# Eight-row blocks for the triangular inverse on VectorE, several operations merged, and a new written order of the work

## The chip, the cores and the metric

One core of one Trainium2 chip runs the whole program. The metric is the time of one execution on the device in microseconds; lower is better. The core has four engines that matter here: TensorE (PE in the profile; its weight loads are PEld), VectorE (DVE), ScalarE (ACT) and GpSimd (POOL). SyncE (SP) issues most of the transfers from and to HBM. Each engine works through its own instructions strictly in the order in which they were written.

## The reference

A recurrent attention (a state of 40 x 40 for each of 32 pairs of batch and head, 768 steps) is followed by a mixture of 8 experts with one expert per row:

```python
for t in range(S):                       # B, H, S, D = 4, 8, 768, 40
    y[:, :, t] = einsum('bhd,bhde->bhe', r_t, state)
    Sa = einsum('bhde,bhe->bhd', state, a_t)
    state = state * w_t[:, :, None, :] - einsum('bhd,bhe->bhde', Sa, b_t)
    state = state + einsum('bhd,bhe->bhde', v_t, k_t)
x = y as rows of 320 (3072 of them)
expert = argmax(x @ w_gate)              # with a softmax weight for the row
h = max(x_rows_of_expert @ w1[e], 0)     # 320 -> 1024, at most 768 rows per expert
out[row] = weight * (h @ w2[e])          # 1024 -> 320
```

All inputs and the result are float32.

## The kernel before, in words

The 768 steps are cut into six passes (`i` from 0 to 5) of 128 steps, and each pass into two chunks of 64 (`c`). Heads are packed in two groups (`pr` 0 and 1), so each pass has four units (`pr`, `c`). Inside a chunk the 64 steps do not follow one another in time: the effect of `Sa` within a chunk is a lower triangular system of 64 x 64 for every head, and the kernel inverts that triangle.

**The steps of one pass.** `decay` and `decay_k` turn the factors `w` into running products by two scans on VectorE (L518, L527) and multiply them into `a` and `kb` (L532 and L537, on VectorE or on GpSimd). `nn` forms the triangles by matmul (L418, operands `a` and `kb`) and copies them, negated, from PSUM into `ns` (L161). `inverse` then works on the two 32 x 32 diagonal blocks of each triangle, with the 32 triangles of the pass side by side:

- L792 transposes `ns` into `xu`, so that each partition holds a whole 32 x 32 block in its 1024 elements, and VectorE can work along the partition.
- The elimination (L665 and L670, function `elim`) goes row by row through the two diagonal blocks of 16: a product of a column of `xu` with a row of `nu` into `tmp`, then a sum into `nu`. For rows with much work it is cut into two halves, listed as `inverse` and `inverse_b`, which do not depend on one another.
- Two transposes (L680, L685) bring the result back.
- `join` takes the blocks from 16 to 32 by two rounds of matmuls (`yb`, `yq` and `sw` are their operands; L736, function `take_jb`, puts the corner into `xu`), and `comb` takes them from 32 to 64 in the same way. The result is `nt`.

`chain` is the recurrence: `zz` and `chain` compute `Sa` from the state `D` or `E`, `uT`, `out` and `turn` compute the outputs and the new state. In `out` the matmuls of step `yy` take two products into one PSUM tile, one with `bk` and one with `Sd`, the turned state. `take_y` scales the output into `px` (L982) and `gate` makes the rows of 320 as a float16 pair, high and low, in `x16`, and the logits of the router. `route` makes the lists of rows, and the expert steps (`x`, `w`, `p`, `h`, `o`) gather rows and multiply by the weights; these are the last 214 us.

**What sets the order.** Every step has a function, the engines that it may run on with planned durations ("V1.97", "A.62 A.62|V.69 V.69"), and the steps and buffers that it needs. The order is not planned when the program is built: the table `ORDER` at L31 lists the steps one by one. A name is the next step of that thread, `/1` chooses the second engine, `*2` repeats, and `~3` puts three idle matmuls of 128 x 512 (function `warm`, L210) ahead of it, which fill a gap on TensorE. The buffers are few: `ns`, `xu`, `nu`, `yb` and `yq` exist once, so the inverse of one pass has to be finished with them before the next one starts.

## Time and profile before

| | us |
|---|---|
| median of 3 runs (606.46 to 618.24) | 613.48 |
| the profiled execution | 609.18 |
| its span from first to last instruction | 606.9 |
| recurrence, up to the first expert's matmuls | 0 to 393 |
| experts alone | 393 to 606.9 |

Busy time is the time in which an engine had at least one instruction; the remaining time it waited. The granted clock of TensorE was 0.975 of full speed over the span. The six inverses start (L792) at 31.8, 76.7, 134.0, 189.6, 251.3 and 308.8 us, so the passes between them took 44.9, 57.3, 55.6, 61.7 and 57.5 us.

### The profile page before, as it was taken

What the parts mean: (1) busy time and instruction counts of PE and PEld (TensorE: products, weight loads), DVE (VectorE), ACT (ScalarE), POOL (GpSimd) and SP (SyncE); (2) the same over time, 40 slices, a digit from 0 to 9 for tenths busy, and PEclk for the clock granted to TensorE, in tenths of its full rate; (3) what the DMA queues carried; (4) which work ended last, traced back from release to release, by engine and by line L of the source; (5) the groups of instructions that cost most, each with busy time, mean ns of one, the idle gap of its engine ahead of it and who ended that gap; (6) DMA issues with size and microseconds to landing.
All of it is one profiled execution on the core that took longest, in us unless ns stands there. A gap on an engine that the chain in (4) does not pass through costs nothing.

```text
span 606.9 us, 25053 instructions
## 1 busy us (share of the span) xinstructions
PE 529.7 (87%) x11167; PEld 388.4 (64%) x11167; DVE 423.5 (70%) x904; ACT 291.7 (48%) x544; POOL 156.8 (26%) x184
## 2 busy tenths in 40 slices
PE   0576789889988988998889999799899998999995
PEld 0344478778866876887678788566565553655653
DVE  6998988979897886799799489477247252551540
ACT  3133646664656476556556653165336442452431
POOL 9110003240330154111320000303422333451323
PEclk9998999999999998999899999799799998999999
DMA  7672015413630455134332422886798589693211
GB/s 227 201 227 62 2 33 161 150 53 122 191 123 12 145 157 167 53 113 153 105 98 74 150 73 60 172 199 201 197 230 185 149 199 237 161 245 88 46 55 48
DMA packets 74761, 80.82 MB, mean 133 GB/s; under 512 B 31550, under 2 KB 55232, under 8 KB 74644
## 3 DMA queue, kind: packets, MB, share of 16 engines
q1 hardware_dynamic: 71316, 69.69, 41.6%
q0 software_dynamic: 3328, 9.44, 5.8%
q8 instruction: 89, 1.46, 1.0%
q14 instruction: 28, 0.23, 0.1%
HBM read 64.16 MB, written 10.09 MB: 122 GB/s over the span
## 4 chain that ended last, share of the span: by engine, by line
PE 41%; DVE 22%; issue 13%; ACT 10%; DMA 7%; POOL 3%; SPq 2%; another core or an unknown queue 1%; POOLq 0%; DVEq 0%; ACTq 0%
PE pp L418 19%; PE pp L1632 8%; PE p L1501 5%; ACT yb L161 3%; DMA xT<-a 3%; POOL out_dram L1507 2%; DVE tmp L665 2%; DVE nu L670 2%; DVE vu L470 2%; PE pp L888 2%; PE pp L210 2%; DVE px L527 2%; DVE ns L161 1%; ACT ns L161 1%; DVE xu L736 1%
## 5 line engine op out<-in xcount | busy, mean ns | idle before, releaser
L1507 POOL DMA_INDIRECT out_dram<-tk,ri x27 | 36.1, 1336 | 103.0 <-ACT tk L1667 82.0
L418 PE MATMUL pp<-a,kb 64*64 64x64 f32 x1536 | 32.4, 227 | 24.7 <-DVE a L532 20.1
L210 PE MATMUL pp<-ident 128*128 128x512 f16 x146 | 40.8, 388 | 10.0 <-ACT ns L161 2.2
L418 PEld LDWEIGHTS pp<-a,kb 64*64 64x64 f32 x1536 | 27.5, 139 | 32.5 <-issue 27.9
L466 POOL TENSOR_SCALAR_AFFINE_SELECT tk<-tk 64x512 f32<-64x512 f32 x24 | 15.8, 657 | 103.8 <-ACT tk L463 102.8
L418 PE MATMUL pp<-vu,bk 128*40 128x104 f32 (+1 forms) x768 | 39.2, 254 | 3.3 <-issue 2.6
L537 POOL TENSOR_TENSOR kb<-kb,gx 104x1024 f32<-104x1024 f32 x13 | 29.0, 2239 | 47.1 <-DVE nu L670 18.9
L418 PEld LDWEIGHTS pp<-vu,bk 128*40 128x40 f32 x768 | 33.6, 118 | 8.4 <-issue 5.9
L1478 POOL DMA_INDIRECT a<-xd,ri x25 | 26.2, 1049 | 45.9 <-DVE gs L1393 27.9
L1640 DVE SCALAR_TENSOR_TENSOR px<-pp,rv 128x448 f16<-128x448 f32 (+1 forms) x24 | 13.8, 597 | 32.2 <-ACT rv L1637 32.2
L418 PE MATMUL pp<-yb,ns 128*64 128x64 f32 (+1 forms) x768 | 25.8, 228 | 9.5 <-ACT yb L161 9.5
L161 ACT ACTIVATE yb<-nu,few 64x512 f32<-64x512 f32 (+1 forms) x36 | 29.7, 857 | 8.8 <-DVE nu L685 8.2
L161 ACT ACTIVATE ns<-pp 32x256 f32<-32x256 f32 (+1 forms) x42 | 18.9, 451 | 30.9 <-PE pp L418 30.2
L157 ACT COPY vT<-pp 128x1024 f32<-128x1024 f32 x22 | 22.3, 1014 | 23.0 <-PE pp L888 20.8
L418 PEld LDWEIGHTS pp<-yb,ns 128*64 128x64 f32 (+1 forms) x768 | 24.0, 131 | 12.8 <-ACT yb L161 12.1
L527 DVE TENSOR_TENSOR_SCAN px<-px,z 104x1032 f32<-104x1032 f32 x12 | 31.3, 2606 | 0.4
L1632 PE MATMUL pp<-xT,px 128*128 128x448 f16 (+2 forms) x128 | 29.1, 315 | 2.4 <-issue 1.8
L470 DVE TENSOR_TENSOR vu<-pp,mask 128x1024 f32<-128x1024 f32 x22 | 26.8, 1218 | 6.2 <-PE p L926 3.7
L1632 PE MATMUL pp<-xT,xu 128*128 128x448 f16 (+2 forms) x128 | 28.5, 315 | 2.7 <-DMA xT<-a 2.7
L1637 ACT ACTIVATE rv<-pp 128x448 f16<-128x448 f32 (+2 forms) x28 | 13.1, 490 | 36.1 <-PE pp L1632 29.0
L418 PE MATMUL pp<-rv,vT 64*64 64x64 f32 x1536 | 28.4, 221 | 2.2 <-ACT vT L157 1.2
L518 DVE TENSOR_TENSOR_SCAN gx<-px,z 104x1032 f32<-104x1032 f32 x12 | 27.7, 2308 | 3.4 <-DMA px<-in_w_dram 2.7
(262 smaller groups left out, 1433.7 us busy)
## 6 DMA issues: line engine op xcount, KB each, us to landing
vu<-in_moe_w_dram SPq DMA_DIRECT2D x32, 320.0 KB
kb<-in_kb_dram SPq DMA_DIRECT2D x40, 224.0 KB
px<-in_moe_w_dram SPq DMA_DIRECT2D x16, 512.0 KB
rv<-in_rv_dram SPq DMA_DIRECT2D x24, 256.0 KB
vu<-in_vt_dram SPq DMA_DIRECT2D x48, 128.0 KB
xd<-x SPq DMA_DIRECT2D x24, 192.0 KB
a<-in_a_dram SPq DMA_DIRECT2D x16, 224.0 KB
px<-in_moe_w_dram SPq DMA_DIRECT2D x14, 256.0 KB
```

The costliest lines, as they stand in the source:

```text
L157: (e.copy if e is self.nc.scalar else e.tensor_copy)(out, in_)
L161: (e.mul if e is self.nc.scalar else e.tensor_scalar_mul)(out, in_, x)
L210: self.nc.tensor.matmul(x, self.spare[:, 0:P], self.spare[:, None, :].to_broadcast([P, 2, 2 * P]), start=True, stop=True, skip_group_check ...
L418: TT.matmul(out, l, r, start=start, stop=True, skip_group_check=True)
L470: V.tensor_mul(out, in_, m.to_broadcast(sh))
L518: V.tensor_tensor_scan(T["gx"][0:R, 0:H * (P + 1)][:, ::-1], T["px"][0:R].rearrange("p h t -> p (h t)")[:, ::-1], z2[0:R].rearrange("p h t ...
L527: V.tensor_tensor_scan(T["px"][0:R].rearrange("p h t -> p (h t)"), T["px"][0:R].rearrange("p h t -> p (h t)"), z2[0:R].rearrange("p h t -> ...
L537: engine().tensor_mul(x, x, g[:, :, None, half(c)].to_broadcast([R, H, 2, C]))
L1478: nc.gpsimd.indirect_dma_start(out=xt(j)[:c].rearrange("p a c -> p (a c)"), out_offset=None, in_=src[:, :], in_offset=bass.IndirectOffsetO ...
L1501: nc.tensor.matmul(po[z], h(l, f + z), rr(f + z, 1)[:, 0], start=(f == 0 and m == 0), stop=(f == NF - n and m == 2), skip_group_check=True)
L1507: nc.gpsimd.indirect_dma_start(out=out_v[used[0] % (8 * E)][:, :], out_offset=bass.IndirectOffsetOnAxis(ap=ri.bitcast(U32)[:c, j, 1:2], ax ...
L1632: nc.tensor.matmul(s_["h", f + z][:, :n], l, rr, start=m % 7 == 0 and m < 14, stop=m >= 14)
```

## The change: smaller blocks, merged operations, another order

What it does, by part:

1. The elimination covers four diagonal blocks of 8 instead of two of 16: six rows of a product and a sum on all four blocks at once, uncut, in place of fourteen rows, most of them cut in two. `inverse_b` is gone.
2. From 8 to 16, VectorE forms the corner itself: two products of 512 elements and a sum over groups of 8, twice (`corner_mul`, `corner_sum`). It uses the buffer `yq` for the products.
3. Pairs of instructions become one: `take_jb` (with another placing of `join_b`'s output in PSUM), `take_turn` (the copy into `Sd`), `take_y`, and the high half in `x_hi`. The factor 64 moves from `take_y` to `x_hi` and `x_lo`.
4. In `yy` the product with `Sd` goes first and the one with `bk` second.
5. `ORDER` is new from end to end, with its choices of engine and its idle matmuls (146 + 28 before, 148 + 21 now).

```diff
 ORDER = """
-load_w decay0 load_kb decay0 load_a decay_k0 load_kb load_a load_w decay_k0 decay1 load_kb inverse_0 load_kb
...
+load_kb load_w decay0 load_kb load_a decay0 load_rv load_kb load_w decay_k0 load_a load_kb inverse_0 load_w decay_k0
...
-        nb = 2 if i in SIX else 1
-        ne = 32 // nb
+        nb, ne = 4, 8
...
-            m = s + 1
-            rows = [(s + 1, ne)]
-            if nb * (ne - 1 - s) * m >= 84:
-                h = s + 1 + (ne - s) // 2
-                rows = [(s + 1, h), (h, ne)]
...
+            m, n = s + 1, ne - 1 - s
+            tv = tmp[:, 0:nb * n * m].rearrange("p (b t j) -> p b t j", b=nb, t=n)
+
+            def mul():
+                V.tensor_mul(tv, diag(s_["xu"])[:, :, s + 1:, s:s + 1].to_broadcast([P, nb, n, m]),
+                             diag(s_["nu"])[:, :, s:s + 1, 0:m].to_broadcast([P, nb, n, m]))
+
+            def add():
+                y = diag(s_["nu"])[:, :, s + 1:, 0:m]
+                V.tensor_add(y, y, tv)
+
+            return mul, add
+
+        def eight(x, b, t, s, *dims):
+            return skew(x, b * 528 + t * 32 + s, *dims)
+
+        def corner_mul(x):
+            def go():
+                if x == 0:
+                    s_["y"] = get("yq")
+                for b in range(2):
+                    if x == 0:
+                        l = eight(s_["xu"], b, 8, 0, (32, 8), (0, 8), (1, 8))
+                        r = eight(s_["nu"], b, 0, 0, (0, 8), (1, 8), (32, 8))
+                    else:
+                        l = eight(s_["nu"], b, 8, 8, (32, 8), (0, 8), (1, 8))
+                        r = skew(tmp, P + 64 * b, (0, 8), (1, 8), (8, 8))
+                    V.tensor_mul(flat(s_["y"])[:, 512 * b:512 * b + 512].rearrange("p (t j s) -> p t j s", t=8, j=8), l, r)
+            return go
+
+        def corner_sum(x):
+            def go():
+                y = flat(s_["y"])
+                if x == 0:
+                    V.tensor_reduce(tmp[:, P:], y.rearrange("p (m s) -> p m s", s=8), AX.X, ALU.add)
+                else:
+                    V.tensor_reduce(skew(s_["nu"], 256, (528, 2), (32, 8), (1, 8)),
+                                    y.rearrange("p (b t j s) -> p b t j s", b=2, t=8, j=8), AX.X, ALU.add)
+                    put("yq", s_["y"])
+            return go
...
-            for z in range(2):
-                x = s_["ntd"][half(z), :, 16:32].rearrange("p (v u) t -> p v u t", v=2)
-                y = s_["p"][half(z), ::1 - 2 * z, 0:256].rearrange("p v (u t) -> p v u t", u=16)
-                V.scalar_tensor_tensor(x, y, low[half(z), 0:1], x, ALU.mult, ALU.add)
+            x = s_["ntd"][:, :, 16:32].rearrange("p (v u) t -> p v u t", v=2)
+            y = s_["p"][:, :, 0:256].rearrange("p v (u t) -> p v u t", u=16)
+            V.scalar_tensor_tensor(x, y, low, x, ALU.mult, ALU.add)
...
+        for x in range(2):
+            add(corner_mul(x), "V1.2", take=["yq"] * (1 - x))
+            add(corner_sum(x), "V1.2", free=["yq"] * x)
...
-            for x in range(2):
-                copy(U["Sd"][:, x], pv[:, :, C * x:C * x + D])
+            copy(U["Sd"], skew(U["pd"], 0, (C, 2), (R, 4), (1, D)))
...
-            for r in range(2):
-                x = T["px"][0:R, 4 * r:4 * r + 4, ct]
-                y = p[0:R, r].rearrange("p (k y) -> p k y", k=4)[:, :, D * r:D * r + C]
-                V.scalar_tensor_tensor(x, y, SX, x, ALU.mult, ALU.mult)
+            x = T["px"][0:R, :, ct].rearrange("p (r k) t -> p r k t", r=2)
+            V.tensor_mul(x, skew(p[0:R], 0, (512 + D, 2), (P, 4), (1, C)), x)
```

Instructions that the new list puts on another engine or takes from one, counted on VectorE (before, now): `zs` copies 14, 2; `vu` copies 10, 18; `Sd` copies 32 (halves), 4 (whole), with 18 whole ones on ScalarE; `nt` copies from PSUM 10, 4; products of `a` 7, 4 (GpSimd 5, 8); scalings into `yb` 0, 8, into `sw` 0, 2, into `yq` 0, 2; mask products into `tk` 6, 7; `vT` copies 2, 3.

Three places show what the new list moves. In the rows, numbers behind a name are buffers, and line numbers are those of each file.

SP's first transfers, before: `px` is the factor `w` of a group, each row a pair of half transfers.

```order
L171 DMA px_119<-in_w_dram 128x516 x2
L171 DMA kb_129<-in_kb_dram 128x512 x2
L171 DMA a_125<-in_a_dram 128x512 x2
L171 DMA kb_129<-in_kb_dram 128x512 x2
L171 DMA a_126<-in_a_dram 128x512 x2
L171 DMA px_120<-in_w_dram 128x516 x2
L171 DMA kb_130<-in_kb_dram 128x512 x4
```

The same place in the changed kernel:

```order
L157 DMA kb_129<-in_kb_dram 128x512 x2
L157 DMA px_119<-in_w_dram 128x516 x2
L157 DMA kb_129<-in_kb_dram 128x512 x2
L157 DMA a_125<-in_a_dram 128x512 x2
L157 DMA rv_131<-in_rv_dram 128x512 x2
L157 DMA kb_130<-in_kb_dram 128x512 x2
L157 DMA px_120<-in_w_dram 128x516 x2
```

The `w` of the first group has moved from first to second place, and that of the second group from sixth to seventh.

VectorE between the second L685 of pass 0 (after `take_jb`) and the transpose that starts the inverse of pass 1, before:

```order
L161 TENSOR_SCALAR nt_141<-xu_138,few 128x16x32 x2
L525 COPY g_1_165<-gx_118 104x8
L526 RECIPROCAL z_168<-gx_118 104x8
L527 SCALAR_TENSOR_TENSOR px_122<-px_122,z_168 104x1032
L532 TENSOR_TENSOR a_128<-a_128,px_122 104x1024
L537 TENSOR_TENSOR kb_130<-kb_130,gx_118 104x1024 x2
L161 TENSOR_SCALAR ns_137<-pp_113 128x512
L161 TENSOR_SCALAR ns_137<-pp_113 32x8x32 x2
L157 COPY nt_140<-pp_115 32x16x32 x2
```

The same stretch in the changed kernel:

```order
L510 COPY g_1_165<-gx_118 104x8
L511 RECIPROCAL z_168<-gx_118 104x8
L512 SCALAR_TENSOR_TENSOR px_122<-px_122,z_168 104x1032
L147 TENSOR_SCALAR sw_136<-xu_138,few 64x512 x2
L522 TENSOR_TENSOR kb_130<-kb_130,gx_118 104x1024
L147 TENSOR_SCALAR ns_137<-pp_113 128x512
L147 TENSOR_SCALAR ns_137<-pp_113 32x8x32 x2
L147 TENSOR_SCALAR ns_137<-pp_113 128x512
L147 TENSOR_SCALAR ns_137<-pp_113 32x8x32 x2
L503 SCALAR_TENSOR_TENSOR gx_118<-px_123,z_168 104x1032
L143 COPY zs_153<-pp_114 64x8x40 x2
```

The product of `a`, one of `kb`, the two copies into `nt` at either end have left VectorE there; two for `sw` and two for `zs` have come.

GpSimd's first products, before:

```order
L537 TENSOR_TENSOR kb_130<-kb_130,gx_118 104x1024
L537 TENSOR_TENSOR kb_129<-kb_129,gx_118 104x1024
L466 AFFINE_SELECT tk_135<-tk_135 64x512 x4
```

GpSimd's first products in the changed kernel:

```order
L522 TENSOR_TENSOR kb_129<-kb_129,gx_118 104x1024 x2
L517 TENSOR_TENSOR a_127<-a_127,px_121 104x1024
L522 TENSOR_TENSOR kb_130<-kb_130,gx_118 104x1024
L517 TENSOR_TENSOR a_128<-a_128,px_122 104x1024
```

Five products of pass 1 stand there now in place of one (the first of before belongs to pass 0); over the whole program GpSimd has 21 of them where it had 18.

## Rows read from the trace of the kernel before

**Rows 1.** The page's busy times (share, instructions) and the chain by engine.

```profile
PE 529.7 (87%) x11167; PEld 388.4 (64%) x11167; DVE 423.5 (70%) x904; ACT 291.7 (48%) x544; POOL 156.8 (26%) x184
PE 41%; DVE 22%; issue 13%; ACT 10%; DMA 7%; POOL 3%; SPq 2%; another core or an unknown queue 1%; POOLq 0%; DVEq 0%; ACTq 0%
```

**Rows 2.** Stretch, length; busy PE, PEld, DVE, ACT, POOL (instructions); clock, DMA share, GB/s.

```profile
31.77:76.67 44.90, 32.89 (x693) 21.47 (x692) 40.17 (x82) 19.68 (x34) 2.18 (x1) 0.96 0.29 89
76.67:133.95 57.28, 52.50 (x1697) 44.52 (x1697) 48.50 (x107) 34.47 (x64) 15.09 (x12) 1.00 0.34 105
...
393.00:606.90 213.90, 200.12 (x1424) 119.57 (x1421) 95.55 (x174) 89.55 (x170) 68.30 (x58) 0.97 0.65 160
```

**Rows 3.** Groups by line and shape, TensorE: count, busy us, mean ns, idle before.

```profile
L210 PE MATMUL pp<-ident 128*128 128x512 f16 x146 | 40.8, 388 | 10.0 <-ACT ns L161 2.2 <-issue 2.0 <-ACT yq L157 1.2
L418 PE MATMUL pp<-vu,bk 128*40 128x104 f32 x704 | 35.7, 254 | 0.7 <-DVE vu L470 0.5
```

**Rows 4.** VectorE in order of time, start of the program: start, us, instruction.

```profile
4.61 2.31 DVE L518 TENSOR_TENSOR_SCAN gx<-px,z 104x1032 f32<-104x1032 f32 x1 [2.18 <-DMA px<-in_w_dram]
...
14.68 2.31 DVE L518 TENSOR_TENSOR_SCAN gx<-px,z 104x1032 f32<-104x1032 f32 x1 [0.52 <-DMA px<-in_w_dram]
...
19.54 4.05 DVE L527 TENSOR_TENSOR_SCAN px<-px,z 104x1032 f32<-104x1032 f32 x1
...
31.77 1.93 DVE L792 STREAM_TRANSPOSE xu<-ns 128x1024 f32<-128x1024 f32 x1 [0.26 <-ACT ns L161]
```

**Rows 5.** VectorE in order of time, the inverse of pass 0.

```profile
33.96 0.22 DVE L665 TENSOR_TENSOR tmp<-xu,nu 128x56 f32<-128x56 f32 x1
34.22 0.22 DVE L670 TENSOR_TENSOR nu<-nu,tmp 128x56 f32<-128x56 f32 x1
...
38.10 1.23 DVE L470 TENSOR_TENSOR tk<-pp,mask 128x1024 f32<-128x1024 f32 x1
...
40.31 2.23 DVE L665 TENSOR_TENSOR tmp<-xu,nu 128x60 f32<-128x60 f32 x1
...
45.46 1.97 DVE L680 STREAM_TRANSPOSE xu<-nu 128x1024 f32<-128x1024 f32 x1
47.47 1.25 DVE L685 STREAM_TRANSPOSE nu<-xu 128x1024 f32<-128x1024 f32 x1
```

**Rows 6.** GpSimd in order of time, its first two products.

```profile
19.20 2.23 POOL L537 TENSOR_TENSOR kb<-kb,gx 104x1024 f32<-104x1024 f32 x1 [3.66 <-DMA kb<-in_kb_dram]
40.28 2.18 POOL L537 TENSOR_TENSOR kb<-kb,gx 104x1024 f32<-104x1024 f32 x1 [18.85 <-DVE nu L670]
```

**Rows 7.** Groups of VectorE by line and shape: the prices.

```profile
L1370 DVE TENSOR_TENSOR tm<-lane,sp 128x512 f32<-128x512 f16 x5 | 3.4, 684 | 0.0
L1355 DVE TENSOR_TENSOR ne<-ne,oh__99 128x128 f32<-128x128 f32 x1 | 0.4, 393 | 0.0
L1346 DVE TENSOR_TENSOR ne<-p,base 128x128 f32<-128x128 f32 x1 | 0.3, 283 | 0.0
L1302 DVE TENSOR_REDUCE mx<-lg 128x16 f32<-128x128 f32 x1 | 0.3, 286 | 0.0
L157 DVE COPY Sd<-p 128x160 f32<-128x160 f32 x32 | 8.8, 317 | 0.3 <-PE p L926 0.2
L157 DVE COPY zs<-pp 64x320 f32<-64x320 f32 x14 | 6.8, 487 | 1.1 <-PE pp L418 0.8
L527 DVE TENSOR_TENSOR_SCAN px<-px,z 104x1032 f32<-104x1032 f32 x12 | 31.3, 2606 | 0.4
```

**Rows 8.** VectorE in order of time, end of pass 0 and start of pass 1.

```profile
58.16 1.51 DVE L736 SCALAR_TENSOR_TENSOR xu<-pp,few,xu 64x512 f32<-64x512 f32 x2 [1.55 <-PE pp L418]
...
65.43 2.35 DVE L537 TENSOR_TENSOR kb<-kb,gx 104x1024 f32<-104x1024 f32 x2
...
69.43 1.38 DVE L157 COPY nt<-pp 32x512 f32<-32x512 f32 x2
...
76.67 2.00 DVE L792 STREAM_TRANSPOSE xu<-ns 128x1024 f32<-128x1024 f32 x1 [1.07 <-ACT ns L161]
```

More of the change, by code (lines that the diff above doesn't have):

```diff
@@ L796, in inverse @@
         add(begin2, "V1.97", needs=[("nn", (pr, 2 * i + c)) for pr in range(2) for c in range(2)] + [("unit", i)], take=["xu"])
[L797 to L798 removed]
+        add(first, "V.2")
         for s in range(1, ne - 1):
[L800 to L805 removed]
+            for x in elim(s):
+                add(x, "V.2")
+        for x in range(2):
+            add(corner_mul(x), "V1.2", take=["yq"] * (1 - x))
+            add(corner_sum(x), "V1.2", free=["yq"] * x)
         add(back_a, "V1.94", gives=("ntd0", i))
@@ L814, in inverse @@
         add(join_b, "P1.0", needs=[("sw", i)], take=["pp"], free=["yq", "sw"])
[L815 removed]
+        add(take_jb, "V.69", free=["pp"], gives=("ntd", i))
         add(lambda: back_b(0, 1), "V1.22", gives=("n1", i))
@@ L957, in yy @@
                        True)
+            if q:
+                for k in range(4):
+                    for r in range(2):
+                        for x in range(2):
+                            mm(p[half(x, D), r, k * P + D * r:k * P + D * r + C], U["Sd"][half(r), x, k, :],
+                               T["rv"][half(r), c, x * 4 + k, :], k == 0 and not old)
+                put("Sd", U["Sd"])
             for k in range(4):
@@ L1001, in chain @@
             more(turn, "P.4", needs=[("S", pr, q)], take=["p1"], gives=("turned", n))
-            more(take_turn, "A.33 A.33|V.33 V.33", take=["Sd"], free=["p1"], gives=("Sd", n))
+            more(take_turn, "A.46|V.49", take=["Sd"], free=["p1"], gives=("Sd", n))
         more = steps(f"out{pr}")
@@ L1010, in chain @@
                  take=[kind], free=[kind] * (q > 0) + ["g0"] * c, gives=("S", pr, q + 1))
-        more(take_y, "V.36 V.36", free=["pp"], gives=("y", n))
+        more(take_y, "V.66", free=["pp"], gives=("y", n))
     def late(i):
```

230 lines of the change are left out of this document (91 added, 139 removed).

## The prediction

> **What bounds the kernel now.** First the page's busy times and its chain by engine [rows 1]: TensorE is busy for 87% of the span and VectorE for 70%, and the chain that ended last runs 41% through TensorE and 22% through VectorE. That is a mean over parts with different limits, so I cut the span at the transposes that start the inverses [rows 2]. In the first pass (44.9 us) VectorE is busy for 40.2 us and TensorE for 32.9 us; in a later one (57.3 us) VectorE for 48.5 and TensorE for 52.5 us; among the experts TensorE for 200.1 of 213.9 us. So the first pass belongs to VectorE, the last stretch to TensorE, and the passes between to neither alone: TensorE's busy time holds idle matmuls, 146 of 388 ns each over the program [rows 3], that only fill gaps. What sets the length of such a pass is the loop from one inverse to the next through `join`, `comb` and `nn`, which has to share VectorE with everything else. The change touches that loop and VectorE's load. It adds nothing to TensorE's real work, and it leaves the experts as they are but for their order.
>
> **The elimination.** In rows [5] a product, its sum and the next product start 0.26 us apart, each waiting for the one ahead. From the first product at 33.96 to the transpose at 45.46 us there are 11.5 us; 1.2 of them are the mask product at 38.10, and 2.0 an interruption at 40.31 us, where an instruction that takes 0.22 us elsewhere took 2.23 [rows 5]. The work itself is 8.3 us, much of it in halves that overlap. The new one has no halves: 12 instructions in a row at 0.26 us are 3.1 us. Then come the corners: two products of 512 elements, a sum over 1024, and the same again. The lower end of a product is 0.684 us, what 512 elements took [rows 7]. But one operand of each is read with a step (32 floats in the first round, 8 in the second). The transpose at 45.46 us, which writes with a step of 32, took 1.97 us where the one at 47.47 us took 1.25 [rows 5]: 0.70 ns more for each of 1024 elements. The 128-element product at L1355 with a stepped operand took 393 ns where L1346 took 283 [rows 7]: 0.86 ns more. I take 0.75 ns, the middle of the two, so a product is 0.684 + 0.38 = 1.07 us, as these two rows are stepped accesses and the 0.684 one is not. A sum of 128 elements costs 286 ns where an addition of 128 costs 283 [rows 7], so a sum over 1024 is priced like the 1024-element mask product, 1.23 us [rows 5]. New total: 3.1 + 4 x 1.07 + 2 x 1.23 = 9.8 us, against 8.3: **1.5 us longer per inverse**; without the step's price it would be 8.3, no change.
>
> The Trainium skill bears on this: "SBUF — State Buffer", Specifications (TRN2), says that SBUF is read in lines of 16 bytes and that an access pattern needs at least two hits in each line for full bandwidth. By that rule all four products pay and the sum is the 9.8 us; by the plain 512-element row it is 8.3 us, and six inverses differ by 9 us.
>
> **The merged operations.** `take_jb` is two instructions in 1.51 us [rows 8] and becomes one of the same free size, 0.75 us: 0.75 us off the loop, in each pass. `take_turn` on VectorE was 32 copies of 317 ns, 8.8 us; now 4 copies of 320 elements at 0.487 us (the `zs` copy of that size) [rows 7], 1.9 us, since the list gives 18 to ScalarE. That is 6.9 us less on VectorE. Merged `take_y` and `x_hi` save at most the start of an instruction; I count nothing, since the elements stay the same. In `yy` the product with `Sd` can now run while the mask product is awaited; TensorE's whole wait ahead of the product with `bk` is 0.7 us [rows 3], as other matmuls cover it, so this too is nothing; were the cover gone, the product with `Sd` would fill the gap.
>
> **The list.** From the counts of the two orders on VectorE, over the six passes: 12 `zs` copies fewer at 0.487 us (-5.8), 8 `vu` copies of that size more (+3.9), 6 `nt` copies fewer at 0.69 us, half of the pair in [rows 8] (-4.1), 3 products of `a` fewer at 1.2 us, half of the pair of `kb` in [rows 8] (-3.6). Against that come 8 more for `yb`, 2 for `sw` and 2 for `yq`, bounded by the rows of their element counts, 0.684 and 1.23 us (+10.4), and one mask product and one 1024-element copy at 1.23 (+2.5); some 16 small copies go, at 0.28 to 0.49 us (-6). With `Sd` the list takes 9.6 us from VectorE, 1.6 us a pass. ScalarE and GpSimd get part of that; ScalarE was busy for 34.5 of 57.3 us [rows 2] and has room.
>
> **Start.** The first scan starts at 4.61 us and the fifth load after it lets the next group's scan start at 14.68 us [rows 4]: 2.0 us a load. The first `w` moves from first to second place (about 6.6 us), the second from sixth to seventh (16.7 us). But behind that second scan VectorE loses two sets of `ns` copies (to ScalarE, about 1.6 us each) and a stall of 1.7 us in the scan at 19.54 us (4.05 against 2.31 us, with a GpSimd product beside it) [rows 4, 6], and gets one more product of 1.2 us. 31.77 + 2.0 - 3.2 - 1.7 + 1.2 = 30.1 us: **1.7 us earlier**; between 1 later, if the stall stays, and 3 earlier.
>
> **First pass** (VectorE's). Elimination +1.5 and the interruption of 2.0 us gone, since no GpSimd product is listed for that place: -0.5. `take_jb` -0.75. Between it and 76.67 us VectorE has lost a product of `a`, one of `kb`, two `nt` copies (1.2 + 1.2 + 1.4) and a scaling, and got one for `sw` like it and two of 0.487: -2.8, of which I take 2.2, as the last wait there, 1.07 us, is for ScalarE [rows 8]. **-3.5 us**, bounds -6 and -1.
>
> **Each of the five later passes.** +1.5 - 0.75 - 1.6 = -0.85 of VectorE's time; VectorE is busy for 85% of such a pass, so I take 0.7 of it, 0.6 us: **-3 us** for five, bounds +4 (only the loop counts: +0.75 each) and -12 (no price for the step: -2.35 each).
>
> **Sum.** -1.7 - 3.5 - 3.0 = -8.2. The profiled execution took 609.18 us, 2.3 outside its span of 606.9; 609.2 - 8.2 = 601.0. That execution was 4.3 below the median of the runs, 613.48, and from the median it is 605.3. I predict the middle, **603 us**.
>
> **Rivals.**
> - *The step costs nothing.* Then 9 us more are saved, 594 us. The row of 684 ns speaks for it, both stepped rows against. Chance 0.12.
> - *The new list also closes gaps.* In a later pass VectorE idles for 8.8 us and TensorE for 4.8 [rows 2] beside its idle matmuls. Two us a pass closer would give 603 - 10 = 593 us. For it: the list is written for the new durations. Against: it asks for 169 idle matmuls where the old one had 174, so it leaves about as much open. Chance 0.24.
> - *GpSimd holds VectorE up: slower.* Both long VectorE instructions above had a GpSimd product of 2.2 us beside them (19.20 and 40.28 us [rows 6]), and cost 1.7 and 2.0 us more. There were 18 such products, and now there are 21, five of them at once in pass 1's preparation, beside scans and corners. If 14 more than before hit VectorE at 2.0 us, the sum is -8 + 28, some 631 us; it decides the sign from 10 hits on (20 us, against the 8 saved and 12 for 2%). Against it: all twelve scans at L527 average 2606 ns [rows 7], only 3.6 us above 12 x 2.31, so most products of before missed. Chance 0.12. The Trainium skill has it as a rule ("SBUF — State Buffer", SBUF: two separate sides): a VectorE instruction with two SBUF inputs and a GpSimd instruction exclude each other for their whole length. By that rule the corners, which have two such inputs, are open to it too; two rows here agree, the twelve scans show that it is seldom met.
> - *It does nothing in the later passes*, as the recurrence and not the inverse sets them: only start and first pass count, 608 us from the median. Included in the middle.
>
> **Numbers.** A difference of 2% (12 us) is about what a measurement of this kernel can tell, so faster means below 601. The forecast, 597 to 612 us, has 0.48, of which 0.08 lies below 601; with 0.12 and 0.22 of the two better rivals faster has 0.42. Slower has 0.12 from GpSimd and 0.04 for another list whose waits fall badly: 0.16. Within 2%: 0.42. The range goes from 590 (both better rivals in part) to 617 (the upper bounds of the start and the later passes), leaving 0.07 below and 0.14 above.
>
> **What will show it.** Corner products near 1.07 us (or 0.68), sums near 1.23, elimination and corner together near 9.8 us where nothing lies between; the first inverse starting near 30 us, the second near 71.5; later passes of 56 to 57 us; experts still some 214 us. It is wrong if passes change by more than 2 us either way, if the experts' stretch changes, or if VectorE instructions of over 2 us turn up beside GpSimd products.

## The result, and the profile after

The changed kernel took 590.43 us (median of 4 runs, 586.94 to 591.2) where the kernel before took 612.89 in the same set: a ratio of **0.9656 [0.9568, 0.9744]** (it compares only executions in the chip's faster state, so it is not the quotient of the two medians). On a second chip it gave 0.9641 [0.9592, 0.969]. The forecast was 603 us, with a range of 590 to 617: the time lies in the range, but not where the likeliest case had it. It is nearest to the second rival, 593 us ("the new list also closes gaps").

The profiled execution took 590.8 us, its span is 589.1. First the page's busy times:

```profile
PE 521.2 (88%) x11162; PEld 383.8 (65%) x11162; DVE 413.9 (70%) x665; ACT 293.5 (50%) x550; POOL 160.8 (27%) x181
```

VectorE has 239 instructions fewer than in [rows 1], and 9.6 us less to do; the span is 17.8 us shorter. The shares hardly moved, so this view does not say where the time went. The windows do: the five stretches between the starts of the inverses, the last part of the recurrence, and the experts from their first matmul (columns as in [rows 2]).

```profile
31.06:76.30 45.24, 34.82 (x761) 22.32 (x759) 36.92 (x47) 20.63 (x36) 11.25 (x5) 0.96 0.33 102
76.30:132.21 55.91, 52.79 (x1709) 44.84 (x1712) 47.10 (x66) 34.33 (x68) 14.05 (x8) 1.00 0.35 107
132.21:186.60 54.39, 49.82 (x1585) 41.55 (x1580) 45.76 (x61) 35.16 (x69) 12.94 (x11) 1.00 0.43 131
186.60:242.36 55.76, 52.40 (x1736) 44.89 (x1732) 48.63 (x76) 34.01 (x63) 17.56 (x15) 1.00 0.39 122
242.36:297.48 55.12, 49.81 (x1605) 42.38 (x1595) 48.10 (x70) 33.62 (x64) 13.62 (x13) 0.97 0.39 123
297.48:381.80 84.32, 75.78 (x2174) 63.62 (x2173) 73.12 (x156) 36.36 (x69) 10.27 (x10) 1.00 0.33 97
381.80:589.10 207.30, 195.71 (x1421) 118.05 (x1421) 92.80 (x171) 87.50 (x165) 66.68 (x62) 0.99 0.64 167
```

Before, the same seven were 44.9, 57.3, 55.6, 61.7, 57.5, 84.2 and 213.9 us. So the start gained 0.7 us, the first pass nothing (+0.3), the second to fifth pass 11.0 together (5.9 of them in the fourth), the last part nothing, the experts 6.6. These are differences of two single executions. A second profile of the changed kernel (after_again) gave 45.0, 57.8, 54.5, 58.2, 54.6, 84.7 and 207.3 us: a single pass repeats to about 2.5 us, and of the fourth pass's 5.9 us only 3.5 came again.

In the four passes that gained, TensorE is the engine to look at. This is their window, and TensorE's idle matmuls in it, in the kernel before (length 232.16 us, TensorE busy 210.61):

```profile
76.67:308.83 232.16, 210.61 (x6623) 177.02 (x6623) 197.37 (x436) 135.99 (x258) 61.69 (x56) 0.99 0.36 114
L210 PE MATMUL pp<-ident 128*128 128x512 f16 x59 | 17.4, 381 | 3.2 <-issue 2.0 <-DVE vT L157 0.6 <-DVE x L1048 0.5
L210 PE MATMUL p<-ident 128*128 128x512 f16 x20 | 5.9, 382 | 0.0
```

and in the changed kernel (length 221.18, TensorE busy 204.82):

```profile
76.30:297.48 221.18, 204.82 (x6599) 173.67 (x6599) 189.59 (x271) 137.11 (x261) 58.17 (x46) 0.99 0.39 120
L196 PE MATMUL pp<-ident 128*128 128x512 f16 x44 | 13.7, 382 | 0.2 <-DVE x L1040 0.2
L196 PE MATMUL p<-ident 128*128 128x512 f16 x17 | 4.8, 380 | 0.0
```

Time in which TensorE does nothing that counts is its gaps and its idle matmuls: 21.6 + 17.4 + 5.9 = 44.9 us before, 16.4 + 13.7 + 4.8 = 34.9 now. That is **10.0 of the 11.0 us**. The real matmuls took 187.3 us and take 186.3. In the second profile the same sum is 19.3 + 13.7 + 4.8 = 37.8 us, 7.0 less than before, and the four passes are 7.2 us shorter. Note what this does not prove: a stretch is real matmuls, idle matmuls and gaps, so with the real ones unchanged any shortening has to turn up in the other two, whatever caused it.

The granted clock accounts for some of what is left, and of the experts. In the kernel before, TensorE fell to half speed (1.2 of 2.4 GHz) five times after the first pass, leaving out the last 3 us of the span, where it falls in both kernels; two of the stretches:

```profile
296.90:300.30 3.40, 3.40 (x96) 3.15 (x100) 1.01 (x3) 0.73 (x4) 2.04 (x1) 0.51 0.14 39
433.50:440.70 7.20, 6.05 (x39) 4.01 (x39) 4.24 (x11) 3.77 (x11) 0.97 (x2) 0.53 0.18 49
```

In the changed kernel there is one such stretch behind the first pass (288 to 294 us, mean granted clock 0.72), and none among the experts. Which executions fall, and where, varies: with the old list the experts took 213.9, 209.1, 209.1 and 213.4 us in four profiles, with the new list 203.8 to 207.3 in ten.

### The profile page after: what moved, and what is told of

The parts are those of the page before. It is cut to its first block, busy times and chain, and to the rows that moved or that the text cites. A ratio compares the mean times of both kernels' runs of the same rounds, so it can differ in the third digit from the quotient of the medians.

```text
span 589.1 us, 24793 instructions
## 1 busy us (share of the span) xinstructions
PE 521.2 (88%) x11162; PEld 383.8 (65%) x11162; DVE 413.9 (70%) x665; ACT 293.5 (50%) x550; POOL 160.8 (27%) x181
## 4 chain that ended last, share of the span: by engine, by line
issue 20%; PE 15%; DVE 7%; POOL 6%; DMA 4%; ACT 2%; SPq 1%; POOLq 1%; DVEq 0%; ACTq 0%
PE pp L403 5%; PE pp L1624 3%; POOL out_dram L1499 3%; PE p L1493 3%; POOL a L1470 2%; DMA xT<-a 1%; DMA a<-xd,ri 1%; PE pp L885 1%; DMA out_dram<-tk,ri 1%; DVE vu L455 1%; DMA nt<-in_moe_w_dram 1%; DVE yq L661 1%; PE p L1126 1%; PE pp L570 1%; SPq L1609 1%
## 5 line engine op out<-in xcount | busy, mean ns | idle before, releaser
L522 POOL TENSOR_TENSOR kb<-kb,gx 104x1024 f32<-104x1024 f32 x13 | 33.4, 2576 | 80.7 <-DMA kb<-in_kb_dram 47.3
L403 PE MATMUL pp<-a,kb 64*64 64x64 f32 x1536 | 31.3, 229 | 20.9 <-DVE a L517 18.5
L403 PEld LDWEIGHTS pp<-a,kb 64*64 64x64 f32 x1536 | 26.8, 140 | 30.6 <-DVE a L517 21.0
L1470 POOL DMA_INDIRECT a<-xd,ri x26 | 30.3, 1166 | 58.3 <-DVE gs L1385 31.3
L1499 POOL DMA_INDIRECT out_dram<-tk,ri x23 | 25.9, 1126 | 61.3 <-ACT tk L1659 49.4
L517 POOL TENSOR_TENSOR a<-a,px 104x1024 f32<-104x1024 f32 x8 | 17.5, 2182 | 55.6 <-DVE px L512 30.1
L1624 PE MATMUL pp<-xT,z 128*128 128x448 f16 (+2 forms) x128 | 27.7, 306 | 5.4 <-DMA xT<-a 4.3
L1624 PE MATMUL pp<-xT,ns 128*128 128x448 f16 (+2 forms) x192 | 32.1, 306 | 0.0
L143 ACT COPY zs<-pp 64x320 f32<-64x320 f32 x46 | 19.3, 419 | 23.9 <-PE pp L403 23.4
L196 PEld LDWEIGHTS <-ident 128*128 128x128 f16 x169 | 15.0, 100 | 24.1 <-issue 12.0
L451 POOL TENSOR_SCALAR_AFFINE_SELECT tk<-tk 64x512 f32<-64x512 f32 x20 | 14.5, 726 | 57.5 <-ACT tk L448 46.6
L578 ACT ACTIVATE bk<-pp,few 128x320 f32<-128x320 f32 x48 | 22.5, 528 | 14.8 <-PE pp L570 14.5
L403 PEld LDWEIGHTS pp<-rv,vT 64*64 64x64 f32 x1536 | 24.9, 134 | 5.9 <-issue 2.2
```

The costliest lines, as they stand in the source:

```text
L143: (e.copy if e is self.nc.scalar else e.tensor_copy)(out, in_)
L196: self.nc.tensor.matmul(x, self.spare[:, 0:P], self.spare[:, None, :].to_broadcast([P, 2, 2 * P]), start=True, stop=True, skip_group_check ...
L403: TT.matmul(out, l, r, start=start, stop=True, skip_group_check=True)
L522: engine().tensor_mul(x, x, g[:, :, None, half(c)].to_broadcast([R, H, 2, C]))
L578: A.activation(U["bk"][:, x].rearrange("p (a b) d -> p a b d", a=2), U["pi"][:, :, 0:4 * R].rearrange("p a (b y) -> p a b y", y=R)[:, :, : ...
L1470: nc.gpsimd.indirect_dma_start(out=xt(j)[:c].rearrange("p a c -> p (a c)"), out_offset=None, in_=src[:, :], in_offset=bass.IndirectOffsetO ...
```

## The experiments

Twelve kernels were run, the changed kernel once more among them. All ratios are to the kernel before, on the same chip. The names in the expectations: Theory L, the new list brings the gain; O, the cheaper operations; C, TensorE's granted clock; S, VectorE's chain sets a pass; G, GpSimd's products hold VectorE up; T, TensorE's order and gaps set it; R is the rival of T, N and E split the list into order and engines. The last three columns are for the first five passes: length, gaps of TensorE (length less busy, so idle matmuls count as busy), VectorE busy, each from one profile.

| kernel | ratio [95%] | length | gaps | VectorE |
|---|---|---|---|---|
| before | 1 | 277.1 | 33.6 | 237.6 |
| old_list_merged | 1.0003 [0.9954, 1.0053] | 278.1 | 33.2 | 230.4 |
| old_list_eight | 1.0332 [1.0249, 1.0416] | 296.5 | 43.3 | 236.1 |
| old_list_fourth | 1.0087 [1.0051, 1.0123] | 282.1 | 33.6 | 234.3 |
| new_list_old_code | 0.9701 [0.9663, 0.9738] | 274.7 | 31.2 | 224.3 |
| new_list_sixteen | 0.9767 [0.9693, 0.984] | 270.7 | 29.8 | 218.3 |
| the changed kernel | 0.9656 [0.9568, 0.9744] | 266.4 | 26.8 | 226.5 |
| after_again (the same) | 0.9641 [0.9592, 0.969] | 270.1 | 29.5 | 227.4 |
| new_order_old_engines | 1.0348 [1.0275, 1.0422] | 300.9 | 50.4 | 237.9 |
| new_products_dve | 0.9726 [0.9691, 0.9762] | 272.0 | 34.1 | 241.5 |
| kk_twice | 0.9808 [0.9756, 0.9859] | 276.2 | 27.0 | 228.6 |
| new_no_idle | 0.9886 [0.982, 0.9952] | 270.2 | 50.6 | 229.9 |
| corner_rows | 0.9545 [0.9508, 0.9583] | 264.1 | 25.6 | 225.1 |
| corner_rows_first | 0.9523 [0.9477, 0.957] | 261.0 | 24.4 | 225.1 |

**List or operations?** Four kernels split the change. First the merges under the old list, with the old elimination:

```diff
 ORDER = """
+load_w decay0 load_kb decay0 load_a decay_k0 load_kb load_a load_w decay_k0 decay1 load_kb inverse_0 load_kb
...
-        add(first, "V.2")
-        for s in range(1, ne - 1):
-            for x in elim(s):
-                add(x, "V.2")
+        for muls, adds in op[1:]:
+            for x in range(len(muls)):
+                more = add if x == 0 else steps("inverse_b")
+                more(muls[x], "V.2")
+                more(adds[x], "V.2")
```

> The merged operations (take_jb, take_turn, take_y, x_hi, the order inside yy) under the old list, with the old 16-row elimination. Theory L (the new list brought the gain): only take_jb is on the loop, 6 x 0.75 us, so 608 us, and no more than 3 us around it; the experts' stretch stays at 214 us. Theory O (the cheaper operations brought it): at least half of the 22 us, 602 us or less.

1.0003: the merges took 7.2 us of work off VectorE in five passes and nothing off the time that the interval (3 us either way) would show. Then all of the new code under the old list:

```diff
+        work = [x for s in range(1, ne - 1) for x in elim(s)] + [f(x) for x in range(2) for f in (corner_mul, corner_sum)]
+        slots = 28
+        for k in range(slots):
+            z = [work[x] for x in range(len(work)) if x * slots // len(work) == k]
+            add(lambda z=z: [f() for f in z], "V.2")
```

> All of the changed code under the old list: the 18 new instructions of each elimination are spread over the places that the old one had. Theory L: elimination 9.5 us in place of 8.3 per pass, so 0 to 7 us more than old_list_merged, 608 to 615 us. Theory O: 590 to 600 us, as the new kernel.

3.3% slower, more than either theory had: blocks of 8 under a list made for blocks of 16. VectorE in order of time in its fourth inverse shows why (start, us, instruction, idle time before it and what ended it):

```profile
200.66 0.21 DVE L652 TENSOR_TENSOR tmp<-xu,nu 128x60 f32<-128x60 f32 x1
201.75 1.22 DVE L469 TENSOR_TENSOR vu<-pp,mask 128x1024 f32<-128x1024 f32 x1 [0.88 <-PE pp L417]
202.89 0.21 DVE L657 TENSOR_TENSOR nu<-nu,tmp 128x60 f32<-128x60 f32 x1
...
207.96 0.49 DVE L928 TENSOR_TENSOR D<-pp,D 104x320 f32<-104x320 f32 x1 [1.27 <-PE pp L417]
208.37 0.68 DVE L990 TENSOR_TENSOR px<-pp,px 104x512 f32<-104x512 f32 x1
210.11 0.49 DVE L928 TENSOR_TENSOR E<-pp,E 104x320 f32<-104x320 f32 x1 [1.05 <-PE pp L417]
```

Between two short rows of the elimination the list has VectorE wait for matmuls that are not done yet; there is less elimination to cover them with, and the long corner comes behind all of them. From begin2 to the first turned inverse this took 25.6 us, against 19.8 with the merges alone. Then the reverse, the new list with blocks of 16:

```diff
-        for s in range(1, ne - 1):
-            for x in elim(s):
-                add(x, "V.2")
+        work = [x for muls, adds in op[1:] for x in muls + adds]
+        slots = 2 * (ne - 2) + 4
+        for k in range(slots):
+            z = [work[x] for x in range(len(work)) if x * slots // len(work) == k]
+            add(lambda z=z: [f() for f in z], "V.2")
```

> The new list with the old 16-row elimination: its instructions are dealt out over the 16 places of the new one. Theory L: 583 to 593 us, since the elimination is 1.2 us shorter per pass by its rows and nothing else changes. Theory O, in the form that the eight-row blocks are what gained: 600 us or more.

0.9767, 593.2 us: at the upper end of L's range, not O's 600. And last the new list with none of the new operations, on all of the old code:

```diff
 ORDER = """
-load_w decay0 load_kb decay0 load_a decay_k0 load_kb load_a load_w decay_k0 decay1 load_kb inverse_0 load_kb
+load_kb load_w decay0 load_kb load_a decay0 load_rv load_kb load_w decay_k0 load_a load_kb inverse_0 load_w decay_k0
...
-                more = add if x == 0 else steps("inverse_b")
-                more(mul, cost, needs=[("row", i, s - 1, 0)] * x)
+        work = [f for s in range(1, ne - 1) for f in [x[0] for x in elim(s)] + [x[1] for x in elim(s)]]
+        for k in range(16):
+            z = [work[x] for x in range(len(work)) if x * 16 // len(work) == k]
+            add(lambda z=z: [f() for f in z], "V.2")
```

> Only the list is new: blocks of 16 (their 46 instructions dealt over 16 of the 18 places that the new list has for an inverse's VectorE work, as before), and none of the merges: take_jb, take_turn, take_y and x_hi in their old instructions, yy in its old order. With the merges and the blocks of 16 the new list gave 0.9767 [0.9693, 0.984] of the kernel before; the changed kernel gave 0.9641 and 0.9656. Theory T (the list's fit to TensorE makes the gain; VectorE's load doesn't): 0.975 to 0.985, the merges' 7 us of VectorE again worth nothing measurable. Rival O (the cheaper operations are worth something under the list that was made for them): 0.99 to 1.0.

0.9701 was better than theory T gave it: **the list alone brings 3.0 of the 3.5%**. What the operations add to it lies within the intervals (0.9701 [0.9663, 0.9738] against 0.9641 [0.9592, 0.969]). With blocks of 16 (new_list_sixteen) VectorE had 8 to 9 us less to do in the five passes than the changed kernel, and the passes were no shorter. The first five inverses ended 2.3, 2.8, 0.0, 2.2 and 3.0 us sooner after their start than in the changed kernel, and the time from there to `take_jb` was 2.1, 5.4, 0.9, 4.3 and 3.0 us longer. In the first three, VectorE stands idle just ahead of `take_jb`, until TensorE has done `join_b` (3.3, 5.0 and 1.6 us); where the rest went is not shown.

**Order or engines?** In the list, 99 steps that may run on either of two engines have another one than before.

```diff
-decay0 join_sw join decay_k0/1 join~8 decay1 load_kb join decay0/1 join~7
+decay0 join_sw/1 join decay_k0 join~8 decay1 load_kb join decay0 join~7
```

> The changed kernel with its new order and its idle multiplications as they are, but for each step that may run on one of two engines (99 of them differ between the lists) the old list's choice. Theory N (the order of the steps brings the gain): the ratio to the kernel before stays at 0.965 to 0.975, passes of 45, 57, 55, 57, 55 us. Rival E (the choice of engines brings it): most of the gain goes, 0.99 or over, with the fourth pass back at 60 us or more. Order and choice were made together, so something between, 0.975 to 0.99, would say that neither does it alone.

1.0348, on the far side of E: the order alone does not do it. The new order with the old engines is worse than the old kernel, as the old order with the new elimination is; the old order with the new engines was not run. In these two runs the list was good only with the durations and the engines that it was made for.

**Idle matmuls and clock.**

```diff
-iden0~4 kk nn1 inverse*2 iden0 inverse*10 zz0~10 kk/1 load_v inverse load_a inverse iden0~1 inverse iden1~6 iden1
+iden0 kk nn1 inverse*2 iden0 inverse*10 zz0 kk/1 load_v inverse load_a inverse iden0 inverse iden1 iden1
```

> The new kernel without its 169 idle matmuls, which leaves out no work. Theory C (part of the gain is TensorE's granted clock, 0.992 against 0.975, and the idle matmuls hold it up): clock 0.97 or less, some 3.4 us at half speed for each fall, 596 to 605 us. Rival: the idle matmuls only delay, 587 to 592 us at a clock of 0.985 or more.

0.9886 against 0.9641 and 0.9656: without its 169 idle matmuls the changed kernel loses two thirds of its gain (597 us, in the range of theory C). In the second to fifth pass the real matmuls took 197.6 us in place of 186.3 (mean granted clock 0.97 in place of 0.99), the gaps rose to 27.9 us, and the four became 4.3 us longer than in the changed kernel's first profile, 0.5 us than in its second. The profiled execution (594.38 us) is the shortest of the four, which go up to 601.25, so where the rest of the loss lies is not shown. The first pass ran at 0.62 of full speed and took 44.65 us, not longer than with them (45.24): neither TensorE's clock nor its load sets that one.

**The fourth pass.** I took the six products of GpSimd there for the reason of the old list's 61.7 us, and moved two of the pair that comes last to VectorE (against old_list_merged).

```diff
-decay1/1 zz1 comb load_kb decay_k1/1 chain0 decay_k1/1
+decay1 zz1 comb load_kb decay_k1 chain0 decay_k1/1
```

> The merges under the old list (1.0003 of the kernel before), with two of the six products that the fourth pass gives to GpSimd done on VectorE: those of a and of the first kb of the pair that comes last. In the kernel before, GpSimd begins with them at 235.68 when the second scan of px is done and ends the second kb at 242.1, and the nn products and begin2 (251.29) come behind. On VectorE a and the first kb end at about 238.2 while GpSimd does the second kb (235.7 to 237.9): 3.9 us earlier. Theory L (where the list puts these products makes the fourth pass 6 us longer): the fourth pass falls from 62 to 58 or 59 us and the whole by 3 to 4 us, ratio 0.994 to the kernel before. Rival (VectorE, or the order behind it, sets the end of that pass): the fourth pass stays at 61 to 63 us.

This failed: the fourth pass took 64.4 us. VectorE's rows there:

```profile
233.85 2.31 DVE L529 TENSOR_TENSOR_SCAN px<-px,z 104x1032 f32<-104x1032 f32 x1
237.25 1.38 DVE L160 COPY nt<-pp 32x512 f32<-32x512 f32 x2 [1.10 <-PE pp L420]
238.67 0.17 DVE L164 TENSOR_SCALAR lg<-p 128x16 f32<-128x16 f32 x1
238.76 3.20 DVE L534 TENSOR_TENSOR a<-a,px 104x1024 f32<-104x1024 f32 x1
241.88 1.21 DVE L539 TENSOR_TENSOR kb<-kb,gx 104x1024 f32<-104x1024 f32 x1
```

The product of `a` stands in VectorE's order behind copies that wait 1.10 us for TensorE, and GpSimd's product, which I had starting at 235.7, started at 238.69 beside it, so that it took 3.20 us. The pair was done at 243.1 us, 9.2 after the start of the scan of `px`; before it was 8.8. The mechanism was not the one that I had named. The windows give what can be said of the 5.9 us: in the fourth pass of the kernel before TensorE has 5.3 us of gaps, 4.6 of idle matmuls and 3.3 us at half speed, in that of the changed kernel 3.4, 4.4 and none, which is 2.1 us and 1.6; the rest, some 2 us, would be work that lies in other passes now (1801 TensorE records in it before, 1736 now; 6631 and 6635 over the four passes). The half speed need not be the list's doing: in after_again, with the new list, it fell into this pass too. The pass in the kernel before, and in after_again:

```profile
189.58:251.29 61.71, 56.43 (x1801) 47.98 (x1797) 48.66 (x110) 36.52 (x71) 21.45 (x20) 0.97 0.40 124
188.57:246.77 58.20, 54.16 (x1735) 46.40 (x1730) 49.40 (x76) 34.04 (x63) 17.55 (x15) 0.97 0.38 117
```

**GpSimd's products.** All 21 of them on VectorE:

```diff
-zz1 decay1/1 load_rv comb inverse_0 chain1 decay_k1 logie0 chain0 logie1
+zz1 decay1 load_rv comb inverse_0 chain1 decay_k1 logie0 chain0 logie1
```

> The changed kernel with the 21 products of a and kb by the decays that the new list gives to GpSimd done on VectorE, in the same places of the list. Theory G (GpSimd's products hold VectorE up more than they take off it): scans return from 2.43 to 2.31 us, sw from 1.5 to 0.3 us a piece, kb from 1.65 to 1.2; VectorE takes 21 times 1.2 = 25 us of products and gets back 12 times 0.12 + 11 times 0.45 + 2.4 = 9 us: 16 us more work over five passes, and the waits for GpSimd's products (2.18 us each, 4.3 for two) go, so the time stays within 1%. Theory L: with 47 us of work in a 56 us pass VectorE has not room for 3 us a pass more ahead of the nn products, and the time goes up by 5 to 15 us, 1.01 to 1.025 of the changed kernel.

0.9726 is 1.009 of the changed kernel on the same chip: inside the 1% that G allowed, just short of L's 1.01. VectorE's prices became even, and three of the rows say how much GpSimd had cost it (the changed kernel's first, then the one without GpSimd's products):

```profile
L503 DVE TENSOR_TENSOR_SCAN gx<-px,z 104x1032 f32<-104x1032 f32 x12 | 29.2, 2430 | 8.5 <-DMA px<-in_w_dram 6.9 <-DVE z L502 0.5 <-POOL kb L522 0.3
L522 DVE TENSOR_TENSOR kb<-kb,gx 104x1024 f32<-104x1024 f32 x11 | 18.2, 1652 | 0.4 <-POOL gx L427 0.3
L147 DVE TENSOR_SCALAR sw<-xu,few 64x512 f32<-64x512 f32 x2 | 3.0, 1495 | 0.1
```

```profile
L525 DVE TENSOR_TENSOR kb<-kb,gx 104x1024 f32<-104x1024 f32 x24 | 29.0, 1212 | 0.2
L506 DVE TENSOR_TENSOR_SCAN gx<-px,z 104x1032 f32<-104x1032 f32 x12 | 27.7, 2307 | 7.4 <-DMA px<-in_w_dram 7.0
L150 DVE TENSOR_SCALAR sw<-xu,few 64x512 f32<-64x512 f32 x2 | 1.0, 482 | 0.1
```

GpSimd held VectorE up by 11 x 0.44 + 12 x 0.12 + 2 x 1.01 = 8.3 us (of the two scalings into `sw` one took 2.51 us and the other 0.48). Yet 14 to 15 us more on VectorE made the five passes only 2 to 6 us longer, some of it paid back by GpSimd's products no longer being awaited.

**TensorE's work doubled at one place.** The changed kernel once more, as a base, and with the matmuls of `kk` issued twice:

> The changed kernel itself, once more, beside the three variants of it below on one chip, so that their ratios to it need no second chip. Its ratio to the kernel before was 0.9656 [0.9568, 0.9744]; expected 0.96 to 0.975. Between the starts of the inverses 45, 56, 54, 56, 55 us, then 84 for the last part of the scan and 207 for the experts.

```diff
-            for h in range(H):
+            for h in [*range(H)] * 2:
                 for pr in range(2):
```

> The changed kernel with the 32 multiplications of each kk step issued twice into the same place (the second overwrites the first with the same values): TensorE has 12 times 0.69 = 8.3 us more work, 6.9 of it in the first five passes, at places where the list has it wait on nobody in particular. Theory T (TensorE, 240 of 266 to 270 us busy in these passes, is the engine that sets their length, and a better list is one that leaves it fewer gaps): nearly all of it shows, 6 to 8 us, ratio to the kernel before 0.975 to 0.98 where the changed kernel has 0.9641 and 0.9656. Rival R (the crossings between engines set the length and TensorE's 27 to 30 us of gaps take the work in): under 3 us, 0.964 to 0.969.

The added work was larger than I had put it: the group of `a` and `kb` rose from 31.3 us (x1536) to

```profile
L403 PE MATMUL pp<-a,kb 64*64 64x64 f32 x2304 | 44.7, 228 | 26.8 <-DVE a L517 18.2 <-issue 6.5 <-DVE px L975 1.9
```

so 13.4 us were added, not 8.3. The time rose by 0.016 of 612 us, some 10 us: about three quarters of what was added shows, and the gaps stayed at 27 us. Adding 14 to 15 us to VectorE cost 2 to 6, and taking 7 to 9 us off it gave nothing. **R**, under 3 us, is out, and this is nearer to **theory T**. But T is not shown by it. The row above has 6.0 us more of "issue", idle time that nothing in the profile explains, than the group has in the changed kernel (0.5). And some of the time came where TensorE is far from full, in the start, of which it idles for 17 us: there `kk` stands in TensorE's order ahead of the last `nn`, and the first inverse started at 33.63 us in place of 31.06 and 31.28. Work put ahead of what others wait for delays them, whether TensorE is the fullest engine or not.

**A cheaper corner.** Both operands and the result of the four products along rows, sums by three additions:

```diff
-                        l = eight(s_["xu"], b, 8, 0, (32, 8), (0, 8), (1, 8))
-                        r = eight(s_["nu"], b, 0, 0, (0, 8), (1, 8), (32, 8))
+                        l = eight(s_["xu"], b, 8, 0, (32, 8), (1, 8), (0, 8))
+                        r = eight(s_["nu"], b, 0, 0, (0, 8), (32, 8), (1, 8))
...
-                    V.tensor_reduce(tmp[:, P:], y.rearrange("p (m s) -> p m s", s=8), AX.X, ALU.add)
+                z = y.rearrange("p (m s) -> p m s", s=64)
+                V.tensor_add(z[:, :, 0:32], z[:, :, 0:32], z[:, :, 32:64])
+                V.tensor_add(z[:, :, 0:16], z[:, :, 0:16], z[:, :, 16:32])
```

> The changed kernel with the next corner's four products laid out so that both operands and the result run along contiguous rows (t, s, j in place of t, j, s), and each sum over eight as three additions of 512, 256 and 128 elements in place of one reduction of 1024. The four stepped products took 1.05 to 1.10 us; a multiplication of 512 contiguous elements takes 0.684: 4 times 0.4 = 1.6 us less an inverse, and the additions 0.65 + 0.37 + 0.24 = 1.26 against 1.22, 0.1 more for two. So VectorE has 1.5 us less work an inverse, 9 us in all. Theory S (VectorE's chain from begin2 to the first turned inverse sets the pass): each pass and the last part get 1 to 1.5 us shorter, 583 us, 0.985 of the changed kernel. Theory L (the list sets the pass by its crossings of engines, and VectorE idles 7 to 9 us a pass): the gain is mostly lost again at the next wait, 588 to 590 us, 0.995 to 1.0. If the step of 32 bytes costs nothing the products stay at 1.05 us.

The products of the changed kernel, by line and shape, and those of this one:

```profile
L661 DVE TENSOR_TENSOR yq<-nu,tmp 128x512 f32<-128x512 f32 x12 | 12.8, 1103 | 0.2
L661 DVE TENSOR_TENSOR yq<-xu,nu 128x512 f32<-128x512 f32 x12 | 12.2, 1054 | 0.2
```

```profile
L661 DVE TENSOR_TENSOR yq<-xu,nu 128x512 f32<-128x512 f32 x12 | 7.8, 688 | 0.2
L661 DVE TENSOR_TENSOR yq<-nu,tmp 128x512 f32<-128x512 f32 x12 | 7.7, 686 | 0.2
```

The step cost 0.37 and 0.42 us a product. The ratio is 0.9545 against 0.9641 on the same chip, 0.990 of it: between S (0.985) and L (0.995 to 1.0). Against after_again the five passes became 6.0 us shorter, 2.3 of them in the first (42.7 for 45.0), and TensorE's gaps fell by 4.0; against the other profile of the changed kernel they became 2.3 us shorter. The saving was smaller than I had put it, as the additions cost more than the reduction: from begin2 to the first turned inverse it is 1.0 us in the first pass and some 3.5 us over all six. The time fell by some 6 us, so here less work for VectorE was not lost again, unlike the larger saving of new_list_sixteen; why stays open. With the first pass's five GpSimd products on VectorE as well:

```diff
-load_kb decay_k0/1 decay0 join_sw join decay_k0/1 join~8 decay1 load_kb join
+load_kb decay_k0 decay0 join_sw join decay_k0 join~8 decay1 load_kb join
```

> The kernel with the corner's products along rows (0.9545 of the kernel before), and in addition the five products of the first pass that the new list gives to GpSimd done on VectorE in the same places. In the changed kernel the scan of gx took 3.77 us beside one of them, two scalings of sw 3.02 us beside another, and the kernel with all 21 on VectorE had its second inverse at 73.73 where the changed kernel has it at 76.3. Theory G (in the first pass these products cost VectorE more than they save): second inverse at 71 to 72.5 us against 73.41, 583 to 584 us in all, 0.952. Rival: the row layout has taken that gain already, and five products of 1.2 us more on VectorE make the first pass the same or up to 2 us longer, 585 to 587 us.

583.25 us, 0.9523: the fastest of all, though its interval and that of corner_rows overlap. For the first pass the rival was right: it took 42.8 us, as without the move (42.7). The second inverse is earlier, 72.72 for 73.41, only as the first one is (29.95 for 30.68), ahead of which none of the five products lies. In corner_rows, GpSimd's products in this pass cost VectorE more than in the changed kernel, and the pass was no longer for it, since the wait for `join_b` took the delay in (0.60 us of it left, 1.44 without those products):

```profile
46.36 4.13 DVE L512 TENSOR_TENSOR_SCAN px<-px,z 104x1032 f32<-104x1032 f32 x1
...
50.72 4.19 DVE L503 TENSOR_TENSOR_SCAN gx<-px,z 104x1032 f32<-104x1032 f32 x1
55.51 0.75 DVE L738 SCALAR_TENSOR_TENSOR xu<-pp,few,xu 128x512 f32<-128x512 f32 x1 [0.60 <-PE pp L403]
```

## Why the prediction came out as it did

| term | forecast | measured |
|---|---|---|
| elimination and corner, alone | 9.8 us | 9.5 us |
| `take_jb` | 0.75 us | 0.750 us |
| start | -1.7 | -0.7 |
| first pass | -3.5 | +0.3 |
| five later passes | -0.6 each | -1.4, -1.2, -5.9, -2.4, +0.1 |
| experts | 0 | -6.6 |
| sum of these | -8.2 | -17.8 |
| profiled execution | -8.2 | -18.4 |

**The prices were right.** In the first pass the elimination and its corner ran from 33.31 to 44.01 us with one mask product of 1.2 us among them. The sums took 1.214 and 1.220 us for my 1.23, the corner products 1.05 and 1.10 for my 1.07, and not the 0.684 of the rival "the step costs nothing". As forecast, blocks of 8 with their corner cost VectorE more than blocks of 16: 8 to 9 us more in five passes (new_list_sixteen). The Trainium skill's rule ("SBUF — State Buffer", Specifications (TRN2): lines of 16 bytes, two hits wanted in each) agrees with the trace here: along rows the same products took 0.69 us.

**The start** came as forecast but for the end: no scan was held up (the second of `px` took 2.31 us), and the first inverse then waited 1.08 us for ScalarE's `ns`, work that I had taken as gone when it left VectorE.

**The first pass failed at "-2.8, of which I take 2.2"**: less work for VectorE was counted as less time. The work did go, 40.2 us [rows 2] became 36.9, but VectorE's idle time there rose from 4.7 to 8.3. Half of the 8.3 is one wait for `join_b`, which was 1.55 us before [rows 8]; in VectorE's order of time:

```profile
50.43 3.77 DVE L503 TENSOR_TENSOR_SCAN gx<-px,z 104x1032 f32<-104x1032 f32 x1 [0.51 <-DVE z L502]
58.41 0.75 DVE L735 SCALAR_TENSOR_TENSOR xu<-pp,few,xu 128x512 f32<-128x512 f32 x1 [4.20 <-PE pp L403]
...
62.97 3.02 DVE L147 TENSOR_SCALAR sw<-xu,few 64x512 f32<-64x512 f32 x2
```

and GpSimd's products beside them:

```profile
49.86 2.18 POOL L517 TENSOR_TENSOR a<-a,px 104x1024 f32<-104x1024 f32 x1 [2.94 <-DVE px L512]
...
63.02 2.18 POOL L517 TENSOR_TENSOR a<-a,px 104x1024 f32<-104x1024 f32 x1 [6.50 <-DVE px L512]
```

In the kernel before, a product of `kb`, one of `a` and the `sw` copies filled the place of the 4.20 us; they had gone to GpSimd and ScalarE. The interruptions by GpSimd came back as well, elsewhere than in [rows 5]: the scan lost 1.5 us and the first of the two scalings 2.0. With all those products on VectorE the first pass took 43.8 us, 1.2 to 1.4 less, and in the kernel with the cheaper corner the same move gave nothing. So as far as these runs show, GpSimd explains the smaller part of the missing 3.8 us. The Trainium skill's rule on the two engines ("SBUF — State Buffer", SBUF: two separate sides), as the prediction states it, agrees with the scan's row, which has two SBUF inputs; the scaling reads one tile besides its factors, so that statement does not cover its 2.0 us. Over the kernel such delays made 8.3 us, far from the rival's 28.

**The later passes failed at the step "VectorE is busy for 85% of such a pass, so I take 0.7 of it".** VectorE's busy share is no price. It lost 11.0 us of work in five passes and the passes 10.6, which looks like a proof, but 7.2 us less without the list gave nothing, and 8 to 9 us less under the new list nothing more. What brought the gain is the list (0.9701 alone), and where it shows is TensorE: 44.9 us of gaps and idle matmuls in the second to fifth pass became 34.9. Which of the list's moves closed them stays open. I had named that rival, but my argument against it (169 idle matmuls asked for, after 174) counted over the program. Where it matters they fell from 79 to 61; elsewhere they grew.

**The experts** I left unchanged, since the change adds and takes nothing there. Their list is new too, and among them the clock no longer fell. The run old_list_eight tells the two apart: it has the old list there, and its clock did not fall among the experts before the last 5 us. The experts in the kernel before, and there up to those 5 us, of 209.1 in all:

```profile
393.00:606.90 213.90, 200.12 (x1424) 119.57 (x1421) 95.55 (x174) 89.55 (x170) 68.30 (x58) 0.97 0.65 160
412.51:616.00 203.49, 196.66 (x1421) 117.19 (x1421) 95.32 (x174) 89.40 (x169) 67.58 (x57) 1.00 0.71 173
```

So 209.1 us is the old list's time at full clock, 1.8 to 5.3 us more than the ten profiles of the new list. That part is the list's; the other 4.8 us of the 213.9 go with the one execution of before, in which TensorE ran some 10 us at half speed among the experts. The split is an estimate, good to some 3 us: old_list_merged took 209.1 us too, with a fall at the experts' start.

So what came in the later passes was the rival that I had at 0.24. The likeliest case was wrong by 12.6 us, in one term above all (-3 forecast, -11 measured) and in one that I had at zero. All three signs of being wrong that the prediction named came true: passes changed by more than 2 us, the experts' stretch changed, and VectorE instructions of over 2 us turned up beside GpSimd's products. That the rival's own sum, -18.2 us, meets the measured -18.4 is luck: it had 2.2 us too much in the later passes, 3.8 in the first pass and 1.0 in the start, and the experts' 6.6 us, which are in no term of it, make up for them.

## What to carry to other kernels

Before a saving on one engine is counted by its busy share, see whose order the others wait in: here 13.4 us added to TensorE, partly ahead of what others wait for, cost 10, while 14 us added to VectorE cost 2 to 6 in the passes and 7 to 9 us taken from it gave nothing; a saving of some 3.5 us in its corner did show. Count gaps and filler work of that engine by stretch, not over the program. A written order belongs to the durations and engines that it was made for: the new order with the old engines, and the new operations under the old list, were each 3% slower than the old kernel; all together are 3.5% faster.
